# Four of sixteen DMA engines for 256 columns of a weight block, and a result in 16 rows

## The chip, the cores and the metric

The kernel runs on one core of one Trainium2 chip. The metric is the device time of one execution in microseconds; runs are compared by the median. A core has engines that run side by side and wait for one another by semaphores: TensorE (PE, its weight loads shown as PEld), VectorE (DVE), ScalarE (ACT), GpSimd (POOL) and SyncE (SP), which here issues the loads and the store. Transfers are carried by 16 DMA engines. SBUF is the memory of 128 partitions that they fill; PSUM is the memory that TensorE accumulates in.

## The reference

One token, with a gate between an attention block and a gated feed-forward block. All is float32.

```
g = sigmoid(sum(x * gate_w))
a = attention(x @ wq, k_cache, v_cache) @ wo      # 32 query heads, 4 key/value heads, 65536 positions
r = x @ w_r
b = x + sigmoid(r) * ((silu(x @ w_gate) * (x @ w_up)) @ w_down)
out = g * a + (1 - g) * b                          # 1024 numbers
```

With one token the router's choice is always that token. D is 1024, the feed-forward width F is 3584, so `w_down` has 3584 rows of 1024 columns.

## The kernel before

The data are read once, in the order of use, through three SBUF buffers `st` of 128 partitions by 64 KB. For each of four key/value heads there are nine loads of 8 MB (part of `wq`, the keys, the values, part of `wo`); then six loads of 7 MB hold `w_gate`, `w_up` and `w_down`. SP issues a load as soon as the buffer it goes to is free, so the DMA queue always has the next loads in it.

The last two buffers come in pieces, each with a semaphore of its own, so that TensorE can begin on a piece before the rest has landed. `ENDS` lists the columns at which pieces end, in units of D = 1024 columns for one block of `w_down`. The last buffer holds blocks 14 to 27: pieces of six blocks, four, two (24 and 25), one (26), then 768 and 256 columns of block 27. Each piece is one DMA of all 128 partitions (line 132). In SBUF the partition p of block b holds row 32 b + p mod 32 of the p // 32-th quarter of `w_down`'s rows.

TensorE works in column groups of 32: four matmuls that write PSUM partitions 0, 32, 64 and 96 on. `hp` is the transposed hidden vector, 32 columns for each block, of which the first has the numbers. Blocks 0 to 23 are added up in the bank `att` (line 392), 512 columns a matmul; after the mark "early" VectorE adds `att` to the attention part in `att_sb` (line 277). The last four blocks (24 to 27, from `EARLY` on) go to banks `y` and `acc` (line 409): `PIECES` splits each quarter of 256 columns into 192 and 64, and a block has four matmuls of 192 columns into `y` and four of 64 into `acc`, one for each group of 32 partitions. In block 26 the matmuls of line 404 add `att_sb` to the same banks, with the weight `halves` that sums the groups; before them TensorE waits for VectorE's sum. The host lays block 27 out so that its first 768 columns hold the `y` part of all four quarters and its last 256 the `acc` part.

When the 192-column part of block 27 is done (mark "first"), ScalarE copies `y` to `fin` (line 182); when the rest is done (mark "last"), VectorE copies `acc` to `fin` (line 280). SP waits for both, stores `fin` as four rows of 256 numbers, from partitions 0, 32, 64 and 96 (line 136), waits until the store has landed, and clears the semaphores.

Instructions of TensorE are laid out in a straight line, but for a loop over the four heads. A matmul of the program appears in the profile as two MATMUL and two LDWEIGHTS records.

Of the kernel before, what the change touches and what calls it, by code (L numbers as in the profile page):

```python
# [4 lines left out]
AF = mybir.ActivationFunctionType  # L5
# [3 lines left out]
P = 128  # L9
D = 1024  # L10
G = 4
# [3 lines left out]
F = 3584  # L15
CH = 8192
NCH = SK // CH
NM = CH // 512
NB = CH // P
KB = D // P  # L20
NQ = D // 4
FB = F // P
FN = F // 8
SCALE = DH ** -0.5
# [3 lines left out]
PER = UNITS // 2  # L28
BUFS = 3

TAIL = 14336
NTAIL = 3 * KB * F // TAIL

ENDS = {NTAIL - 2: [8 * D, TAIL], NTAIL - 1: [6 * D, 10 * D, 12 * D, 13 * D, 13 * D + 768, TAIL]}

PIECES = [(0, 192), (192, NQ)]

EARLY = 24


HEAD = ["q", "qt"] + [f"s{c}" for c in range(NCH)] + ["mx"] + [f"v{c}" for c in range(NCH)] + ["o", "w"]
MARKS = ["dot"] + [f"{m} {g}" for g in range(G) for m in HEAD]
MARKS += ["gate 0", "gate 1", "up 0", "up 1", "early", "first", "last"]
MARK = {m: i + 1 for i, m in enumerate(MARKS)}

LAST = ["s0", "s2", "s4", "s6", "v0", "v2", "v4", "v6", "w"]

ACTS = ["sig"] + [f"{m}{c} {g}" for g in range(G) for m in "se" for c in range(NCH)] + ["hid", "first"]
ACTED = {m: i + 1 for i, m in enumerate(ACTS)}


def gated_mix_kernel(nc, x, vecs, heads, ffn, out):

# [18 lines left out]
    pe, act, dve, pool, sp = nc.tensor, nc.scalar, nc.vector, nc.gpsimd, nc.sync  # L74

    stream = [nc.alloc_sbuf_tensor(f"st{b}", [P, 2 * CH], F32, align_bytes=256)[:, :] for b in range(BUFS)]
    scores = nc.alloc_sbuf_tensor("s", [P, NCH, 512], F32)[:, :, :]
    pts = nc.alloc_sbuf_tensor("pt", [P, 2, 512], F32)[:, :, :]

    hid = scores[:, 0:2, :].rearrange("p a n -> p (a n)")[:, : FB * 32]  # L80
    hp = scores[:, 2:4, :].rearrange("p a n -> p (a n)")[:, : FB * 32]
    att_sb = scores[:, 4, :]
    zeros = scores[:, 5, :]
    fin = scores[:, 7, :NQ]

    o_sb = scores[:, 0, :].rearrange("p (s d) -> p s d", s=4)
    q_sb, lb = scores[:, 1, :], scores[:, 2, :P]
# [1 line left out]
    def sb(name, *shape):  # L89
        t = nc.alloc_sbuf_tensor(name, [P, *shape], F32)  # L90
        return t[tuple(slice(None) for _ in range(len(shape) + 1))]
# [1 line left out]
    xk = sb("xk", 3, KB)  # L93
    x_row, ident, ones, md = sb("x_row", 2 * NQ), sb("ident", P), sb("ones", P), sb("md", P)
    sel, sel8, nsel, sel4 = sb("sel", 32), sb("sel8", HG), sb("nsel", HG), sb("sel4", 4)
    half, halves = sb("half", 2), sb("halves", 2, 32)
    xp, qp, op = sb("xp", KB, 32), sb("qp", 4 * (32 + HG)), sb("op", HG, 32)
    dots, dsum, sig, rest = sb("dots", 2, KB), sb("dsum", 2), sb("sig", 2), sb("rest", 2)
    mx, sums, mh, rl = sb("mx", NCH), sb("sums", NCH), sb("mh", HG), sb("rl", HG)
    m1, nb, l1 = sb("m1", 1), sb("nb", 1), sb("l1", 1)  # L100
    gate = sig[:, 0:1]

    def psum(name, *shape):
        return nc.alloc_psum_tensor(name, [P, *shape])[tuple(slice(None) for _ in range(len(shape) + 1))]

    ps_u, ps_f = psum("ps_u", 2, 512), psum("ps_f", 2, 512)
    ps_s = [ps_u[:, i, :] for i in range(2)]
    acc, ps_m, att, y = psum("acc", 512), psum("ps_m", P), psum("att", 512), psum("y", NQ)

    banks = [y, acc]  # L110

    names = ["done", "fed", "x0", "x1", "x2", "acted", "pooled", "marked", "d2p", "d2a", "d2s", "self"]
    names += [f"ld{b}" for b in range(BUFS)] + [f"end{i}" for i in range(sum(map(len, ENDS.values())))]
    sems = {n: nc.alloc_semaphore(n) for n in names}
# [4 lines left out]
    ends = []  # L119
    for i in range(G * PER + NTAIL):  # L120
        b = i % BUFS
        if i >= BUFS:
            g, l = divmod(i - BUFS, PER)
            sp.wait_ge(sems["marked"], MARK[f"{LAST[l]} {g}" if g < G else ["gate 0", "gate 1", "up 0"][l]])
        if i < G * PER:
            sp.dma_start(stream[b], heads[i]).then_inc(sems[f"ld{b}"], 16)
        elif i - G * PER not in ENDS:
            sp.dma_start(stream[b][:, :TAIL], ffn[i - G * PER]).then_inc(sems[f"ld{b}"], 16)
        else:
            cuts = ENDS[i - G * PER]  # L130
            for c0, c1 in zip([0] + cuts, cuts):
                sp.dma_start(stream[b][:, c0:c1], ffn[i - G * PER, :, c0:c1]).then_inc(sems[f"end{len(ends)}"], 16)  # L132
                ends.append((i, c0, c1))
    sp.wait_ge(sems["acted"], ACTED["first"])
    sp.wait_ge(sems["d2s"], 1)
    sp.dma_start(
        out.rearrange("(j n) -> j n", j=4), fin[::32, :]
    ).then_inc(sems["done"], 16)
    sp.wait_ge(sems["done"], 16)
    sp.sem_clear(range(nums[0], nums[-1] + 1))  # L140

# [4 lines left out]
    for t in (xp, qp, zeros, halves, op):  # L146
# [4 lines left out]
        out=ident, in_=ident, compare_op=ALU.not_equal, fill=1.0, base=0, pattern=[[-1, P]], channel_multiplier=1  # L151
# [3 lines left out]
    acted = []  # L155

    def tell(ins, name):
        acted.append(name)
        return ins.then_inc(sems["acted"])
# [17 lines left out]
            )  # L177
    act.wait_ge(sems["marked"], MARK["gate 1"])
    tell(act.activation(hid.rearrange("p (e n) -> p e n", e=2), ps_f[:, :, :FN], AF.Exp, scale=-1.0), "hid")  # L179
    act.wait_ge(sems["marked"], MARK["first"])  # L180
    c0, c1 = PIECES[0]
    tell(act.activation(fin[:, c0:c1], banks[0][:, : c1 - c0], AF.Copy), "first")
    assert acted == ACTS


# [35 lines left out]
    then(dve.tensor_copy(sel4, ident.rearrange("p (j h) -> p j h", h=32)[:, :, 0]))  # L221

    then(dve.tensor_add(half, sel4[:, :2], sel4[:, 2:]))
    dve.tensor_copy(halves[:, :, 0], half)
    then(dve.tensor_reduce(sel8, ident.rearrange("p (a h) -> p h a", h=HG), AX.X, ALU.add))
    then(dve.tensor_scalar_mul(nsel, sel8, -SCALE))
    for g in range(G):
# [10 lines left out]
        for c in range(NCH):  # L238
            acted_on(f"s{c} {g}")
            ins = dve.tensor_reduce(mx[:, c : c + 1], scores[:, c, :], AX.X, ALU.max)  # L240
# [35 lines left out]
    after("early")  # L276
    to_pe(dve.tensor_add(att_sb, att, att_sb))
    after("last")
    c0, c1 = PIECES[1]
    dve.tensor_copy(fin[:, c0:c1], banks[1][:, : c1 - c0]).then_inc(sems["d2s"])  # L280


    marks = []
# [1 line left out]
    def mark(ins, name):  # L285
        marks.append(name)
        ins.then_inc(sems["marked"])
# [17 lines left out]
    with pe.Fori(0, G):  # L305
        loaded(0)
        for k in range(KB):
            for f in range(2):
                j = 2 * (k % 2) + f
                ins = pe.matmul(  # L310
                    ps_s[0][32 * j : 32 * j + 32, :], xp[:, k, :],
                    unit(0)[:, k * D + f * 512 : k * D + (f + 1) * 512], start=(k < 2), stop=(k >= KB - 2),
                )
        mark(ins, "q")
        take("d2p")
        for e in range(4):
            ins = pe.matmul(ps_m[:, 2 * e : 2 * e + 2], q_sb[:, e * DH : (e + 1) * DH], half, start=True, stop=True)
        mark(ins, "qt")
        take("d2p")
        for c in range(NCH):  # L320
# [3 lines left out]
            for s in range(4):  # L324
                for j in range(4):
                    ins = pe.matmul(  # L326
                        ps_s[c % 2][32 * j : 32 * j + 32, :], qp[:, 32 * s : 32 * s + 32],
                        unit(1 + c)[:, (4 * s + j) * 512 : (4 * s + j + 1) * 512], start=(s == 0), stop=(s == 3),
                    )
# [3 lines left out]
        for c in range(NCH):  # L333
            loaded(1 + NCH + c)
            take("d2p")
            for m in range(NM):
                j = m % 4
                ins = pe.matmul(  # L338
                    acc[32 * j : 32 * j + 32, :], pts[:, c % 2, 32 * m : 32 * m + 32],
                    unit(1 + NCH + c)[:, m * 512 : (m + 1) * 512], start=(c == 0 and m < 4),  # L340
                    stop=(c == NCH - 1 and m >= NM - 4),
                )
# [3 lines left out]
        for s in range(4):  # L346
            ins = pe.matmul(
                ps_m[:, HG : 2 * HG], o_sb[:, s, :], sel[:, HG * s : HG * s + HG], start=(s == 0), stop=(s == 3)
            )
        mark(ins, "o")  # L350
        take("d2p")
        for h in range(HG):
            for f in range(2):
                j = 2 * (h % 2) + f
                ins = pe.matmul(  # L355
                    att[32 * j : 32 * j + 32, :], op[:, h, :],
                    unit(UNITS - 1)[:, h * D + f * 512 : h * D + (f + 1) * 512], start=False, stop=False,
                    skip_group_check=True,
                )
# [4 lines left out]
    def tail(first, n):  # L364
        i, c = divmod(first, TAIL)
        assert c + n <= TAIL
        if i < min(ENDS):
            if c == 0:
                take(f"ld{(G * PER + i) % BUFS}", 16)
        else:  # L370
            for e, (i1, c0, _) in enumerate(ends):
                if (i1 - G * PER, c0) == (i, c):
                    pe.wait_ge(sems[f"end{e}"], 16)
        return stream[(G * PER + i) % BUFS][:, c : c + n]


    for i, part in enumerate(("gate", "up")):
        ps = (ps_f, ps_u)[i]
        for k in range(KB):
            for e in range(2):  # L380
                for j in range(4):
                    ins = pe.matmul(  # L382
                        ps[32 * j : 32 * j + 32, e, :FN], xp[:, k, :], tail((i * KB + k) * F + (2 * j + e) * FN, FN),
                        start=(k == 0), stop=(k == KB - 1),
                    )
# [3 lines left out]
    for b in range(EARLY):  # L389
        for f in range(2):  # L390
            j = 2 * (b % 2) + f
            ins = pe.matmul(  # L392
                att[32 * j : 32 * j + 32, :], hp[:, 32 * b : 32 * b + 32], tail(2 * KB * F + b * D + f * 512, 512),
                start=(b < 2), stop=(b >= EARLY - 2),
            )
    mark(ins, "early")
    for b in range(EARLY, FB):
        if b == EARLY + 2:
            take("d2p")
        for bank, (c0, c1) in zip(banks, PIECES):  # L400
            n = c1 - c0
            for j in range(4):
                if b == EARLY + 2:
                    pe.matmul(  # L404
                        bank[32 * j : 32 * j + 32, :n], halves[:, j // 2, :],
                        att_sb[:, j % 2 * NQ + c0 : j % 2 * NQ + c1], start=False, stop=False,
                    )
                at = 4 * c0 + j * n if b == FB - 1 else j * NQ + c0
                ins = pe.matmul(  # L409
                    bank[32 * j : 32 * j + 32, :n], hp[:, 32 * b : 32 * b + 32], tail(2 * KB * F + b * D + at, n),  # L410
                    start=(b == EARLY), stop=(b == FB - 1),
                )
            if b == FB - 1:
                mark(ins, "first" if c0 == 0 else "last")
    assert marks == MARKS


# [29 lines left out]
```

## Time and profile before

| what | value |
|---|---|
| median of 3 runs | 805.84 us (805.73 to 806.34) |
| profiled execution | 805.78 us |
| its span, first to last instruction | 804.5 us |
| PE busy | 407.5 us, 51% of the span |
| DVE busy | 72.3 us, 9% |
| ACT busy | 44.8 us, 6% |
| DMA | 346.20 MB, mean 430 GB/s |
| granted TensorE clock, mean | 0.75 of full |

The page is of one profiled execution; its time is a little longer than its span, since the time counts what lies before the first and after the last instruction. Busy shares tell little alone: the engine or queue that is behind at the end of a chain of waits sets the time. Three views are used below. The timeline lists groups of instructions: start, duration, engine, line, operation, the tiles it writes and reads, its shapes, the count, and in brackets the idle time before and what ended it. The view of windows gives for each stretch the busy time of PE, PEld, DVE, ACT and POOL, the granted clock, the share of the 16 DMA engines that is busy, and GB/s. The DMA view gives for a stretch, by queue, the packets that start in it, their megabytes, and their time as a share of 16 engines over the stretch; in a stretch shorter than a packet that share can be far over 100%. A DMA of many rows becomes packets, one for each row, and one tiny packet on each engine that tells of its completion. The queue q1 carries SP's loads and the store, q10 the two small loads at the start, and q8 fetches instructions.

### The profile page before, as it was taken

How to read it: one execution, taken by the hardware profiler on the slowest of the kernel's cores; microseconds unless marked ns; L12 is line 12 of the kernel's file. 1: busy time of each engine (PE TensorE's matmuls, PEld its weight loads, DVE VectorE, ACT ScalarE, POOL GpSimd, SP SyncE). 2: the span in 40 equal slices, each digit the busy share in tenths (PEclk: the TensorE clock that was granted, in tenths of full speed). 3: DMA queues.
4: the chain of work that ended last, by engine and by line, in shares of the span. 5: the costliest groups of instructions: out<-in, count | busy, mean ns of one | idle time of the engine just before them, and what ended most of it. 6: DMA issues, size and time to landing. Idle time of an engine off the chain costs nothing. (4 is left out here: it accounts for less than half of the span.)

```text
span 804.5 us, 6124 instructions
## 1 busy us (share of the span) xinstructions
PE 407.5 (51%) x2826; PEld 122.0 (15%) x2826; DVE 72.3 (9%) x135; ACT 44.8 (6%) x100; POOL 2.5 (0%) x13
## 2 busy tenths in 40 slices
PE   0544464455654564545544454456444545464466
PEld 0211111111111121111111111112111111121122
DVE  0200010000000020000100110000000100000310
ACT  0000030000000030000000110000000300000000
POOL 1000000000000000000000000000000000000000
PEclk9977767768767677677877586777776866787778
DMA  9999999999999999999999999999999999999998
GB/s 418 417 418 466 415 424 460 417 428 453 420 430 450 424 431 446 427 430 446 427 430 443 430 430 443 430 431 430 440 433 427 443 430 430 429 448 426 439 413 342
DMA packets 7078, 346.20 MB, mean 430 GB/s; under 512 B 918, under 2 KB 1050, under 8 KB 1308
## 3 DMA queue, kind: packets, MB, share of 16 engines
q1 hardware_dynamic: 6920, 346.04, 99.4%
q8 instruction: 8, 0.13, 0.1%
q10 hardware_dynamic: 148, 0.02, 0.0%
q14 instruction: 2, 0.02, 0.0%
HBM read 346.05 MB, written 0.00 MB: 430 GB/s over the span
## 5 line engine op out<-in xcount | busy, mean ns | idle before, releaser
L326 PE MATMUL ps_u<-st,qp 128*32 128x512 f32 x1024 | 152.5, 759 | 149.1 <-PEq L290 149.1
L338 PE MATMUL acc<-st,pt 128*32 128x512 f32 x1024 | 152.3, 757 | 144.1 <-PEq L290 144.1
L338 PEld LDWEIGHTS acc<-st,pt 128*32 128x32 f32 x1024 | 43.5, 135 | 250.0 <-issue 250.0
L326 PEld LDWEIGHTS ps_u<-st,qp 128*32 128x32 f32 x1024 | 41.4, 135 | 256.3 <-issue 256.3
L171 ACT ACTIVATE s<-ps_u 128x512 f32<-128x512 f32 x32 | 19.1, 597 | 560.4 <-PE ps_u L326 560.4
L240 DVE TENSOR_REDUCE mx<-s 128x1 f32<-128x512 f32 x32 | 22.0, 686 | 284.2 <-ACT s L171 284.2
L255 DVE STREAM_TRANSPOSE pt<-s 128x512 f32<-128x512 f32 x32 | 22.7, 711 | 198.0 <-PE acc L338 194.4
L310 PE MATMUL ps_u<-st,xp 128*32 128x512 f32 x128 | 23.3, 893 | 22.1 <-PEq L290 22.1
L382 PE MATMUL ps_u<-st,xp 128*32 128x448 f32 x128 | 17.1, 703 | 16.9 <-PEq L290 16.9
L382 PE MATMUL ps_f<-st,xp 128*32 128x448 f32 x128 | 16.8, 691 | 13.3 <-PEq L290 13.3
L176 ACT ACTIVATE s<-s,nb 128x512 f32<-128x512 f32 x32 | 22.6, 708 | 10.4 <-DVE nb L250 10.4
L392 PE MATMUL att<-st,s 128*32 128x512 f32 x96 | 14.9, 776 | 7.5 <-DMA st<-in_ffn 4.9
L355 PE MATMUL att<-st,op 128*32 128x512 f32 x128 | 14.6, 594 | 2.4 <-PEq L290 2.4
L301 PE MATMUL ps_m<-dsum,ones 128*128 128x2 f32 x2 | 0.6, 350 | 23.5 <-PEq L290 23.5
L310 PEld LDWEIGHTS ps_u<-st,xp 128*32 128x32 f32 x128 | 5.9, 158 | 40.1 <-issue 40.1
L382 PEld LDWEIGHTS ps_u<-st,xp 128*32 128x32 f32 x128 | 5.3, 139 | 28.6 <-issue 28.6
L259 DVE COPY s<-acc 128x512 f32<-128x512 f32 x4 | 2.8, 692 | 71.6 <-PE acc L338 71.6
L382 PEld LDWEIGHTS ps_f<-st,xp 128*32 128x32 f32 x128 | 5.2, 135 | 25.1 <-issue 25.1
L229 DVE COPY s<-ps_u 128x512 f32<-128x512 f32 x4 | 2.8, 692 | 53.5 <-PE ps_u L310 53.5
L179 ACT ACTIVATE s<-ps_f 128x896 f32<-128x896 f32 x1 | 0.9, 917 | 105.4 <-PE ps_f L382 105.4
L392 PEld LDWEIGHTS att<-st,s 128*32 128x32 f32 x96 | 3.7, 134 | 18.6 <-issue 10.7
L332 PE MATMUL ps_m<-md,ones 128*128 128x128 f32 x8 | 1.8, 311 | 8.2 <-PEq L290 8.2
(69 smaller groups left out, 68.9 us busy)
## 6 DMA issues: line engine op xcount, KB each, us to landing
st<-in_ffn SPq DMA_DIRECT2D x4, 7168.0 KB, 43.3
st<-in_ffn SPq DMA_DIRECT2D x2, 3072.0 KB, 37.1
st<-in_ffn SPq DMA_DIRECT2D x1, 4096.0 KB, 34.9
st<-in_ffn SPq DMA_DIRECT2D x1, 2048.0 KB, 36.9
st<-in_ffn SPq DMA_DIRECT2D x1, 1024.0 KB, 38.9
st<-in_heads SPq DMA_DIRECT2D x36, 48.1
st<-in_ffn SPq DMA_DIRECT2D x1, 512.0 KB, 39.7
st<-in_ffn SPq DMA_DIRECT2D x1, 384.0 KB, 40.2
```

Source lines behind the costliest of these rows:

```text
L171: tell(act.activation(scores[:, c, :], ps_s[c % 2], AF.Copy), f"s{c} {g}")
L176: act.activation(t, t, AF.Exp, bias=nb, scale=SCALE, accum_out=sums[:, c : c + 1]), f"e{c} {g}"
L229: to_pe(dve.tensor_copy(q_sb, ps_s[0]))
L240: ins = dve.tensor_reduce(mx[:, c : c + 1], scores[:, c, :], AX.X, ALU.max)
L255: to_pe(dve.transpose(pts[:, c % 2, :], scores[:, c, :]))
L259: to_pe(dve.tensor_copy(o_sb, acc.rearrange("p (s d) -> p s d", s=4)))
L310: ins = pe.matmul(ps_s[0][32 * j : 32 * j + 32, :], xp[:, k, :], unit(0)[:, k * D + f * 512 : k * D + (f + 1) * 512], start=(k < 2), stop= ...
L326: ins = pe.matmul(ps_s[c % 2][32 * j : 32 * j + 32, :], qp[:, 32 * s : 32 * s + 32], unit(1 + c)[:, (4 * s + j) * 512 : (4 * s + j + 1) * ...
L338: ins = pe.matmul(acc[32 * j : 32 * j + 32, :], pts[:, c % 2, 32 * m : 32 * m + 32], unit(1 + NCH + c)[:, m * 512 : (m + 1) * 512], start= ...
L355: ins = pe.matmul(att[32 * j : 32 * j + 32, :], op[:, h, :], unit(UNITS - 1)[:, h * D + f * 512 : h * D + (f + 1) * 512], start=False, sto ...
L382: ins = pe.matmul(ps[32 * j : 32 * j + 32, e, :FN], xp[:, k, :], tail((i * KB + k) * F + (2 * j + e) * FN, FN), start=(k == 0), stop=(k == ...
L392: ins = pe.matmul(att[32 * j : 32 * j + 32, :], hp[:, 32 * b : 32 * b + 32], tail(2 * KB * F + b * D + f * 512, 512), start=(b < 2), stop= ...
```

## The change

The last buffer is cut otherwise. `ENDS` now has pieces of six blocks, four blocks, the first 768 columns of block 24, its last 256 columns, two blocks (25 and 26), and 768 and 256 columns of block 27. The 256 columns of block 24 (`NARROW`) come by two DMAs with one semaphore, of partitions 0 to 123 and of partitions 124 to 127 (`ROWS`); TensorE waits for 32 on it.

The result is summed in one bank `y` of 64 columns. A block now has 16 matmuls of 64 columns: for c in 0 to 3 and each of the four groups of partitions. The weight is the same 32-column window of `hp`, moved by 8 c columns, so that the numbers come to partition 32 j + 8 c. `halves` becomes 64 columns wide with its numbers in column 32, and is moved in the same way. The 16 matmuls that add `att_sb` stand before block 25, behind the wait for VectorE's sum. ScalarE's copy, the mark "first" and one of SP's waits go; VectorE copies 64 columns of `y`; the store has 16 rows of 64 numbers, from every eighth partition. The host lays block 27 out in 16 runs of 64 columns.

```
-ENDS = {NTAIL - 2: [8 * D, TAIL], NTAIL - 1: [6 * D, 10 * D, 12 * D, 13 * D, 13 * D + 768, TAIL]}
-PIECES = [(0, 192), (192, NQ)]
+ENDS = {NTAIL - 2: [8 * D, TAIL], NTAIL - 1: [6 * D, 10 * D, 11 * D - NQ, 11 * D, 13 * D, 13 * D + 12 * NR, TAIL]}
+NARROW, ROWS = (NTAIL - 1, 11 * D - NQ), [(0, 124), (124, P)]
...
-                sp.dma_start(stream[b][:, c0:c1], ffn[i - G * PER, :, c0:c1]).then_inc(sems[f"end{len(ends)}"], 16)
+                for r0, r1 in ROWS if (i - G * PER, c0) == NARROW else [(0, P)]:
+                    sp.dma_start(
+                        stream[b][r0:r1, c0:c1], ffn[i - G * PER, r0:r1, c0:c1]
+                    ).then_inc(sems[f"end{len(ends)}"], 16)
                 ends.append((i, c0, c1))
-    sp.wait_ge(sems["acted"], ACTED["first"])
     sp.wait_ge(sems["d2s"], 1)
-    sp.dma_start(
-        out.rearrange("(j n) -> j n", j=4), fin[::32, :]
-    ).then_inc(sems["done"], 16)
+    sp.dma_start(out.rearrange("(i n) -> i n", i=16), fin[::8, :]).then_inc(sems["done"], 16)
...
-    act.wait_ge(sems["marked"], MARK["first"])
-    c0, c1 = PIECES[0]
-    tell(act.activation(fin[:, c0:c1], banks[0][:, : c1 - c0], AF.Copy), "first")
...
-    dve.tensor_copy(halves[:, :, 0], half)
+    dve.tensor_copy(halves[:, :, 32], half)
...
-    c0, c1 = PIECES[1]
-    dve.tensor_copy(fin[:, c0:c1], banks[1][:, : c1 - c0]).then_inc(sems["d2s"])
+    dve.tensor_copy(fin, y).then_inc(sems["d2s"])
...
-                    pe.wait_ge(sems[f"end{e}"], 16)
+                    pe.wait_ge(sems[f"end{e}"], 16 * len(ROWS) if (i, c) == NARROW else 16)
...
     for b in range(EARLY, FB):
-        if b == EARLY + 2:
+        if b == EARLY + 1:
             take("d2p")
-        for bank, (c0, c1) in zip(banks, PIECES):
-            n = c1 - c0
+            for c in range(4):
+                for j in range(4):
+                    pe.matmul(
+                        y[32 * j : 32 * j + 32, :], halves[:, j // 2, 32 - 8 * c : 64 - 8 * c],
+                        att_sb[:, j % 2 * NQ + c * NR : j % 2 * NQ + (c + 1) * NR], start=False, stop=False,
+                    )
+        for c in range(4):
             for j in range(4):
-                if b == EARLY + 2:
-                    pe.matmul(
-                        bank[32 * j : 32 * j + 32, :n], halves[:, j // 2, :],
-                        att_sb[:, j % 2 * NQ + c0 : j % 2 * NQ + c1], start=False, stop=False,
-                    )
-                at = 4 * c0 + j * n if b == FB - 1 else j * NQ + c0
+                at = 4 * c + j if b == FB - 1 else 4 * j + c
                 ins = pe.matmul(
-                    bank[32 * j : 32 * j + 32, :n], hp[:, 32 * b : 32 * b + 32], tail(2 * KB * F + b * D + at, n),
-                    start=(b == EARLY), stop=(b == FB - 1),
+                    y[32 * j : 32 * j + 32, :], hp[:, 32 * b - 8 * c : 32 * b - 8 * c + 32],
+                    tail(2 * KB * F + b * D + at * NR, NR), start=(b == EARLY and c == 0),
+                    stop=(b == FB - 1 and c == 3),
                 )
-            if b == FB - 1:
-                mark(ins, "first" if c0 == 0 else "last")
+    mark(ins, "last")
```

More of the change, by code (lines that the diff above doesn't have):

```diff
@@ L21 @@
 NQ = D // 4
+NR = NQ // 4
 FB = F // P
@@ L42 @@
 MARKS = ["dot"] + [f"{m} {g}" for g in range(G) for m in HEAD]
-MARKS += ["gate 0", "gate 1", "up 0", "up 1", "early", "first", "last"]
+MARKS += ["gate 0", "gate 1", "up 0", "up 1", "early", "last"]
 MARK = {m: i + 1 for i, m in enumerate(MARKS)}
 LAST = ["s0", "s2", "s4", "s6", "v0", "v2", "v4", "v6", "w"]
-ACTS = ["sig"] + [f"{m}{c} {g}" for g in range(G) for m in "se" for c in range(NCH)] + ["hid", "first"]
+ACTS = ["sig"] + [f"{m}{c} {g}" for g in range(G) for m in "se" for c in range(NCH)] + ["hid"]
 ACTED = {m: i + 1 for i, m in enumerate(ACTS)}
@@ L83, in gated_mix_kernel @@
     zeros = scores[:, 5, :]
-    fin = scores[:, 7, :NQ]
+    fin = scores[:, 7, :NR]
     o_sb = scores[:, 0, :].rearrange("p (s d) -> p s d", s=4)
@@ L95, in gated_mix_kernel @@
     sel, sel8, nsel, sel4 = sb("sel", 32), sb("sel8", HG), sb("nsel", HG), sb("sel4", 4)
-    half, halves = sb("half", 2), sb("halves", 2, 32)
+    half, halves = sb("half", 2), sb("halves", 2, 64)
     xp, qp, op = sb("xp", KB, 32), sb("qp", 4 * (32 + HG)), sb("op", HG, 32)
@@ L107, in gated_mix_kernel @@
     ps_s = [ps_u[:, i, :] for i in range(2)]
-    acc, ps_m, att, y = psum("acc", 512), psum("ps_m", P), psum("att", 512), psum("y", NQ)
-    banks = [y, acc]
+    acc, ps_m, att, y = psum("acc", 512), psum("ps_m", P), psum("att", 512), psum("y", NR)
     names = ["done", "fed", "x0", "x1", "x2", "acted", "pooled", "marked", "d2p", "d2a", "d2s", "self"]
@@ L430 @@
     down = a["B_w_down"].reshape(4, FB, 32, D).transpose(0, 2, 1, 3).reshape(P, FB, D).copy()
-    last = down[:, -1].reshape(P, 4, NQ)
-    down[:, -1] = np.concatenate([last[:, :, c0:c1].reshape(P, -1) for c0, c1 in PIECES], axis=1)
+    down[:, -1] = down[:, -1].reshape(P, 4, 4, NR).transpose(0, 2, 1, 3).reshape(P, D)
     ffn = np.concatenate([t.reshape(P, -1) for t in (a["B_w_gate"], a["B_w_up"], down)], axis=1)
```

## The prediction

> **What bounds the kernel now.** I read the page's first three parts, then the end of the chain of waits, the timeline of the last 8 us, and the DMA view over ever smaller windows.
>
> ```profile
> span 804.5 us, 6124 instructions
> ...
> DMA  9999999999999999999999999999999999999998
> ...
> q1 hardware_dynamic: 6920, 346.04, 99.4%
> q8 instruction: 8, 0.13, 0.1%
> ```
>
> The load queue (q1) keeps the 16 DMA engines busy for 99.4% of the span, so all of it is a stream of 346 MB, and only what the stream takes, or what follows its last byte, is in the time. The chain says the same, then a short tail:
>
> ```profile
> 760.52 38.89 DMA st<-in_ffn
> ...
> 802.20 0.16 PE acc L409 x8
> 802.36 0.02 issue
> 802.38 0.23 DVE s L280
> ```
>
> The timeline of the tail shows which piece each group of matmuls waited for:
>
> ```profile
> 799.01 0.69 DVE L277 TENSOR_TENSOR s<-att,s 128x512 f32<-128x512 f32 x1 [20.00 <-PE att L392]
> 799.46 0.53 PE L409 MATMUL y<-st,s 128*32 128x192 f32 x8 [0.51 <-DMA st<-in_ffn]
> ...
> 799.80 0.29 PE L409 MATMUL acc<-st,s 128*32 128x64 f32 x8
> ...
> 799.92 0.51 PE L409 MATMUL y<-st,s 128*32 128x192 f32 x8
> ...
> 800.72 0.11 PEld L409 LDWEIGHTS y<-st,s 128*32 128x32 f32 x1 [0.26 <-DMA st<-in_ffn]
> ...
> 801.67 0.53 PE L409 MATMUL y<-st,s 128*32 128x192 f32 x8
> ...
> 802.02 0.29 PE L409 MATMUL acc<-st,s 128*32 128x64 f32 x8
> 802.27 0.33 ACT L182 ACTIVATE s<-y 128x192 f32<-128x192 f32 x1 [58.66 <-PE y L409]
> 802.38 0.23 DVE L280 COPY s<-acc 128x64 f32<-128x64 f32 x1 [2.68 <-PE acc L409]
> 802.70 0.63 SPq L136 DMA_DIRECT2D out<-s  x1
> ```
>
> A piece lands about 0.05 us before the matmuls that it releases: the 1 MB of blocks 24 and 25 at 799.4, block 26 at 800.7, the first 768 columns of block 27 at 801.6, the last 256 columns some 0.3 us on, 801.9. From the last matmuls (802.02) on the tail is fixed: copy, store, end at 804.5.
>
> A landing is that of the slowest engine, and the engines don't end together:
>
> ```profile
> 799.80:800.20 0.40, 0.40 (x24) 0.36 (x16) 0.00 (x0) 0.00 (x0) 0.00 (x0) 1.00 0.88 341
> 800.20:800.60 0.40, 0.40 (x18) 0.23 (x8) 0.00 (x0) 0.00 (x0) 0.00 (x0) 1.00 0.58 228
> 800.60:801.00 0.40, 0.40 (x10) 0.26 (x12) 0.00 (x0) 0.00 (x0) 0.00 (x0) 1.00 0.49 195
> 801.00:801.40 0.40, 0.40 (x18) 0.34 (x11) 0.00 (x0) 0.00 (x0) 0.00 (x0) 1.00 0.41 146
> 801.40:801.80 0.40, 0.40 (x24) 0.39 (x19) 0.00 (x0) 0.00 (x0) 0.00 (x0) 1.00 0.25 77
> ```
>
> The last columns are the granted clock, the DMA share and GB/s. From 800.2 the share falls to 0.58, then 0.49 and 0.41: of 16 engines about nine, eight and seven still move data. Seven to nine have nothing left for up to 1.6 us before the end; the others set it. The window from 801.36 to 801.65 counts the late ones, since an engine ends each piece with one tiny packet:
>
> ```profile
> DMA packets 28, 0.04 MB, mean 125 GB/s; under 512 B 7, under 2 KB 27, under 8 KB 27
> ```
>
> Seven such packets: seven late engines. Why they are late is seen where an instruction fetch (16 KB, q8) meets a load. The rows are the windows 46.35 to 46.45, 47.305 to 47.315 and, undisturbed, 48.35 to 48.37:
>
> ```profile
> q8 instruction: 1, 0.02, 57.8%
> ...
> q1 hardware_dynamic: 1, 0.07, 1828.1%
> ...
> q1 hardware_dynamic: 1, 0.07, 755.6%
> ```
>
> A share times its window times 16 is a packet's time: 0.92 us for the fetch, 2.93 us for the 64 KB packet that follows, against 2.42 us for an undisturbed one. That packet starts at 47.31, 0.91 us behind the fetch, and takes 0.51 longer: one fetch puts one engine back by 1.4 us. Eight fetches, the last at 801.4 when little was left, and seven late engines: each fetch hit another engine.
>
> **The change part by part.** The stream's order and bytes stay. What moves is which engine carries 128 KB of it: 128 rows of 1 KB, 256 columns of block 24, now in DMAs of 124 and of four rows. How many engines these use is to be read from DMAs of few rows. The two-row load of x (window 24.49 to 24.60) and the four-row store (803 to 804.5):
>
> ```profile
> q10 hardware_dynamic: 2, 0.00, 9.3%
> ...
> DMA packets 8, 0.00 MB, mean 3 GB/s; under 512 B 4, under 2 KB 8, under 8 KB 8
> ```
>
> Two packets for two rows, and four packets with four completions for four: an equal share of rows for each engine, at most 16 engines. 124 is four times 31, with no other even split between four and 16, so I take four engines of 31 rows, and the same four with one row each. Bounds: all 16 (nothing changes), or one engine with all 128.
>
> [...]
>
> The price of a row is in the window 801.465 to 801.535, where only 1 KB packets start:
>
> ```profile
> q1 hardware_dynamic: 4, 0.00, 16.4%
> ```
>
> 16.4% of 70 ns on 16 engines is 184 ns, 46 ns for each of four packets, overlapping slightly. The last piece, eight rows an engine, takes 0.3 us, which is 38 ns a row. The four engines carry 32 rows instead of eight: 24 more, 0.9 (38 ns) to 1.1 us (46 ns); I take 1.0. The other twelve carry eight rows less: 0.3 us sooner from there on. If the four are among those that end 1.0 us or more before the last, the landing of every later piece comes 0.3 us sooner.
>
> Which engines these are, the profile doesn't number. Followed from packet to packet (each begins as the one before ends), the two engines of the two-row load are not among those that a q8 fetch hit, as far as packets a few ns apart can be told apart. [...] I take it that the four have the room.
>
> *Issue.*
>
> ```profile
> 759.67 2.70 SPq L132 DMA_DIRECT2D st<-in_ffn  x6
> ```
>
> SP issues eight DMAs where there were these six, two more of 0.45 us each. They stand in one stretch near 760, and the last landed 39 us later (the chain's DMA step), so this hides behind the queue; without that cover it would be 0.9 us. Nothing else waits behind them on SP but the store.
>
> *Matmuls.* The row starts give 0.46 us for a block of four matmuls of 192 and four of 64 columns (799.46 to 799.92), and 0.12 us for four of 64 (799.80 to 799.92). A block is now 16 of 64: four sets, 0.48 us, 0.02 more. The 16 matmuls that add the attention part replace eight, again 0.48 for 0.46, and stand before block 25 instead of inside block 26. They wait for VectorE's sum (799.70); behind them wait blocks 25 to 27. The new 2 MB piece (blocks 25 and 26) lands with the old block 26 less 0.3, at 800.4, so these 0.48 us have 0.7 to fit in; without this cover they cost up to 0.5. Then blocks 25 and 26 run in one go, 0.96 us from 800.43 to 801.39; the 768-column piece is there at 801.35, three sets end at 801.75; the last piece is there at 801.6. So the last four start at 801.75 instead of 802.02, 0.27 sooner: TensorE is just behind the loads, as it was. All of this is at clock 1.00.
>
> *Copies.* ScalarE's copy goes; it ended at 802.60, VectorE's at 802.61, and that one stays 64 columns wide: 0 to 0.02. The wider zeroed weight and its memset lie at the start, under the first load.
>
> *Store.* 16 rows of 256 B for four of 1 KB; by the split above it uses 16 engines. No row shows such a store. Below: packets shorter by 0.03. Above: 16 engines that start from rest, as in the first load, between 1.70 and 2.75, eight of them by 1.90:
>
> ```profile
> DMA packets 8, 0.52 MB, mean 2621 GB/s; under 512 B 0, under 2 KB 0, under 8 KB 0
> ...
> DMA packets 16, 1.05 MB, mean 999 GB/s; under 512 B 0, under 2 KB 0, under 8 KB 0
> ```
>
> Their first packets spread over up to 1.05 us, so up to +0.9. The store has one small packet an engine and its nearest row, the four-row store, is quick: I take +0.1. [...]
>
> *Sum* against the profiled execution, 805.78 us (span 804.5, the rest around it), 0.06 below the median 805.84: 805.78 − 0.27 + 0.1 = 805.6; with the offset, 805.7. From 805.3 (no store cost, full 0.3) to 806.1.
>
> **The rivals.**
> *The four include a late engine.* Then the narrow piece's 1.0 us is put on top of its lateness and all later pieces land that much later: 805.8 + 1.0 + 0.1 = 806.9. For it: seven of 16 are late, and blind chance would seldom leave four free (nine of 16, eight of 15, seven of 14, six of 13: 7%). Against it: the followed pair. Between lie one or two engines that end 0.7 to 0.9 us before the last (the steps from 0.49 to 0.41): with one of these among the four the gain goes, 805.9 to 806.1.
>
> *A fetch lands elsewhere.* TensorE now has twice the matmuls in the last four blocks, so the instruction at which the eighth fetch was sent (801.4, in block 26) is passed in or just behind block 24, about 1.5 us sooner, while data still flow. If it hits one of the four, that engine carries 1.0 and 1.4 us extra on 1.6 of room: the landing comes some 0.8 later, 806.7; on a late engine 1.4 later, 807.3. It decides from the point where the fetch starts before its engine's last packet. Against it: seven fetches went to seven engines, so the eighth should hit one that is early, and most of those aren't among the four.
>
> *It doesn't split as said.* On 16 engines nothing moves: 805.8 to 805.9. On one engine, 128 rows at 38 to 46 ns are 4.9 to 5.9 us, eight rows of which it had before; less 1.6 of room, +3 to +4: about 809.
>
> **How the numbers follow.** Forecast 0.50 (a third of it with the gain lost to a middling engine), late engine among the four 0.24, fetch 0.10, no split 0.06, one engine 0.05, store near its upper bound 0.05 (806.4). Range 805.3 to 807.0: it holds the forecast, the late engine and the dear store, and leaves out most of the fetch on a late engine and the one engine. A measurement of this kernel tells 0.2%, 1.6 us, from no change: faster means under 804.2, which no case reaches (0.03 for a thing not thought of), slower over 807.5, the one-engine case and sums of two others: 0.10. The rest, 0.87, is within.
>
> **What would show it.** Right: four engines seen working alone on 1 KB packets some 2 to 3 us before the end; the DMA share staying near 0.9 up to 801 and falling within half a microsecond; the last matmuls starting near 801.75; from the store's issue to the end the same 1.8 us. Wrong: the share at 0.25 or less for over a microsecond at the end, with the last matmuls past 802.5 (late engine or fetch; a q8 packet before 800.5 tells the second), or the narrow piece landing after the pieces behind it.

## The result, and the profile after

The changed kernel takes 807.45 us (median of 22 runs, 806.48 to 808.09) beside 805.84 us before (22 runs, 805.63 to 806.34). The ratio is 1.0018, with a 95% interval of 1.0013 to 1.0024: slower by 1.6 us, just under the 0.2% that the prediction took as its bound, and above its range. The profiled execution took 807.86 us.

The page's first lines of the changed kernel:

```profile
span 806.5 us, 6284 instructions
...
DMA  9999999999999999999999999999999999999997
...
q1 hardware_dynamic: 7080, 346.04, 99.3%
q8 instruction: 8, 0.13, 0.1%
```

The stream has as many bytes as before, is as dense, and meets eight instruction fetches as before. The 2.0 us that the span has gained are at the end. The chain of waits of the changed kernel (start, duration, what):

```profile
773.11 28.56 DMA st<-in_ffn
801.67 0.04 issue
801.72 1.38 PE y L406 x78
803.10 0.87 issue
803.96 0.51 PE y L406 x18
804.47 0.02 issue
804.50 0.23 DVE s L277
```

Two things are new. The piece of blocks 25 and 26 releases TensorE at 801.72, where 800.43 was forecast. And after 78 of the 96 matmul records of blocks 25 to 27 TensorE stands still for 0.87 us on "issue": it waits for nothing that the profile shows. Record 78 is in the middle of a set of four matmuls, where the program has no wait. VectorE's copy starts at 804.50 where it was 802.38. From the store's issue (804.75) to the end it takes 1.8 us, as before.

The view of windows of the changed kernel, at its end; the last three columns are granted clock, DMA share, GB/s:

```profile
801.40:801.80 0.40, 0.08 (x5) 0.08 (x9) 0.00 (x0) 0.00 (x0) 0.00 (x0) 1.00 0.60 215
801.86:802.16 0.30, 0.30 (x32) 0.30 (x30) 0.00 (x0) 0.00 (x0) 0.00 (x0) 1.00 0.13 48
802.16:802.50 0.34, 0.34 (x40) 0.34 (x32) 0.00 (x0) 0.00 (x0) 0.00 (x0) 1.00 0.07 24
```

Shares of 0.13 and 0.07 are two engines of 16, then one. The other fourteen have ended by 801.87; before, the last of all was through at 801.65, some 0.2 us sooner. So two engines end later than anything did, and the rest have not become earlier.

### The profile page after: what moved, and what is told of

Read it like the earlier page. It is cut to its first block, busy times and chain, and to the rows that moved or that the text cites. A ratio compares the mean times of both kernels' runs of the same rounds, so it can differ in the third digit from the quotient of the medians.

```text
span 806.5 us, 6284 instructions
## 1 busy us (share of the span) xinstructions
PE 399.9 (50%) x2906; PEld 121.3 (15%) x2906; DVE 72.4 (9%) x135; ACT 44.5 (6%) x99; POOL 2.6 (0%) x13
## 5 line engine op out<-in xcount | busy, mean ns | idle before, releaser
L323 PE MATMUL ps_u<-st,qp 128*32 128x512 f32 x1024 | 148.8, 743 | 154.8 <-PEq L287 154.8
L335 PE MATMUL acc<-st,pt 128*32 128x512 f32 x1024 | 149.9, 747 | 146.5 <-PEq L287 146.5
L352 PE MATMUL att<-st,op 128*32 128x512 f32 x128 | 16.3, 652 | 2.4 <-PEq L287 2.4
L352 PEld LDWEIGHTS att<-st,op 128*32 128x32 f32 x128 | 4.9, 117 | 10.4 <-issue 10.4
```

Source lines behind the costliest of these rows:

```text
L323: ins = pe.matmul(ps_s[c % 2][32 * j : 32 * j + 32, :], qp[:, 32 * s : 32 * s + 32], unit(1 + c)[:, (4 * s + j) * 512 : (4 * s + j + 1) * ...
L335: ins = pe.matmul(acc[32 * j : 32 * j + 32, :], pts[:, c % 2, 32 * m : 32 * m + 32], unit(1 + NCH + c)[:, m * 512 : (m + 1) * 512], start= ...
L352: ins = pe.matmul(att[32 * j : 32 * j + 32, :], op[:, h, :], unit(UNITS - 1)[:, h * D + f * 512 : h * D + (f + 1) * 512], start=False, sto ...
```

## The experiments

All runs are compared with the kernel before on the same chip. "Split" stands for the two DMAs of the narrow piece, "pause" for TensorE's stop on "issue" in block 27. A run with fewer causes than the changed kernel is to be read beside the two ends, 805.9 and 807.45.

| run | split 124+4 | pause | median, us | range | before, same chip | ratio, 95% interval |
|---|---|---|---|---|---|---|
| e1 one DMA | no | yes | 806.47 | 806.23 to 806.90 | 805.97 | 1.0007, 0.9997 to 1.0016 |
| e2 split in the kernel before | yes | no | 806.75 | 806.55 to 807.35 | 805.97 | 1.0011, 1.0002 to 1.0020 |
| e3 no pause | yes | no | 806.53 | 806.20 to 807.06 | 805.97 | 1.0007, 0.9998 to 1.0016 |
| e4 one DMA, no pause | no | no | 805.95 | 805.71 to 806.18 | 805.97 | 0.9998, 0.9989 to 1.0007 |
| e5 block 24 early | no | no | 806.30 | 806.07 to 806.79 | 805.85 | 1.0006, 0.9997 to 1.0015 |
| e6 lower and upper half | no | no | 812.91 | 812.72 to 814.67 | 805.85 | 1.0095, 1.0079 to 1.0110 |
| e7 even and odd | no | no | 805.78 | 805.62 to 805.96 | 805.85 | 0.9999, 0.9990 to 1.0008 |
| e9 narrow piece in halves | 64+64 | no | 806.31 | 805.97 to 806.67 | 805.90 | 1.0005, 0.9996 to 1.0014 |
| e10 512 columns | yes | no | 809.34 | 808.31 to 809.75 | 805.90 | 1.0037, 1.0024 to 1.0051 |
| e11 128 columns | yes | no | 805.91 | 805.71 to 806.43 | 805.90 | 1.0001, 0.9992 to 1.0010 |

e8, with the split and a pause, was executed once: 807.09 us. The intervals reach 0.7 us and more to either side, further than most of these runs lie apart; what decides are e1 to e4, which ran side by side on one chip, and the profiles. All eleven executions of e4 (806.18 us at most) are shorter than the shortest of e1, e2 and e3 (806.20).

### e1: one DMA instead of two

```
-NARROW, ROWS = (NTAIL - 1, 11 * D - NQ), [(0, 124), (124, P)]
+NARROW, ROWS = (NTAIL - 1, 11 * D - NQ), [(0, P)]
```

> The changed kernel with the 256 columns of block 24 in one DMA of 128 rows again; matmuls and store as changed. My theory has two causes, each of about 1 us: the split delays the last landing (803.0 for 801.9), and TensorE then runs out of instructions in block 27 (idle from 802.9 to 804.0, in the middle of a set that waits for no load) because its doubled matmuls reach a block of instructions that is still being fetched. So here the last piece lands at 801.8 to 802.2 again, the pause in block 27 stays, and the time is 806.6 to 807.5. Rival, the split alone does it all (the pause too, since the fetch waits on an engine that the split has loaded): 805.7 to 806.0, no pause.

It took 806.47 us, a little under the range of my theory and well over the rival's. The pause is there without the split. Timeline of TensorE in e1:

```profile
801.09 1.34 PE L406 MATMUL y<-st,s 128*32 128x64 f32 x78 [0.25 <-DMA st<-in_ffn]
802.75 0.49 PE L406 MATMUL y<-st,s 128*32 128x64 f32 x18 [0.32 <-issue]
```

The same 78 and 18 records with "issue" between them, but 0.32 us long where it was 0.87. Why it is shorter shows in the last fetch. The first row is the changed kernel's, in a window of 5 ns from 801.350; the second is e1's, in a window of 10 ns from 800.555:

```profile
q8 instruction: 1, 0.02, 1582.5%
...
q8 instruction: 1, 0.02, 576.2%
```

1582.5% of 5 ns on 16 engines is 1.27 us, 576.2% of 10 ns 0.92 us. With the split the fetch begins at 801.35 instead of 800.56 and takes 0.35 us longer. TensorE goes on 1.3 us after the fetch has ended in both: 801.35 + 1.27 to 803.96, 800.56 + 0.92 to 802.75.

### e2: the split alone, in the kernel before

```
-ENDS = {NTAIL - 2: [8 * D, TAIL], NTAIL - 1: [6 * D, 10 * D, 12 * D, 13 * D, 13 * D + 768, TAIL]}
+ENDS = {NTAIL - 2: [8 * D, TAIL], NTAIL - 1: [6 * D, 10 * D, 11 * D - NQ, 11 * D, 13 * D, 13 * D + 768, TAIL]}
+NARROW, ROWS = (NTAIL - 1, 11 * D - NQ), [(0, 124), (124, P)]
...
-                sp.dma_start(stream[b][:, c0:c1], ffn[i - G * PER, :, c0:c1]).then_inc(sems[f"end{len(ends)}"], 16)
+                for r0, r1 in ROWS if (i - G * PER, c0) == NARROW else [(0, P)]:
+                    sp.dma_start(
+                        stream[b][r0:r1, c0:c1], ffn[i - G * PER, r0:r1, c0:c1]
+                    ).then_inc(sems[f"end{len(ends)}"], 16)
...
-                    pe.wait_ge(sems[f"end{e}"], 16)
+                    pe.wait_ge(sems[f"end{e}"], 16 * len(ROWS) if (i, c) == NARROW else 16)
```

> The kernel before with the changed cut of the last buffer and the two DMAs of 124 and four rows; its matmuls of 192 and 64 columns, two copies and four-row store stay. My theory: the last landing is 0.7 to 1.1 us later, no pause of TensorE: 806.5 to 806.9. Rival, the split is hidden or gains and the matmuls and the store do it all: 805.4 to 806.0. Rival, the split does it all: 807.2 to 807.7.

806.75 us, in the first range: 0.8 us over before, with the old matmuls, copies and store. The new cut has a part in it: block 25 now lands with block 26, so that the matmuls of blocks 25 to 27 and the additions among them all stand behind one landing (801.35), where before blocks 24 and 25 were released at 799.46. What the split alone costs is better read from e3 and e4. The copy of `acc` starts at 803.40 (802.38 before), and no matmul waits on "issue":

```profile
803.40 0.23 DVE L285 COPY s<-acc 128x64 f32<-128x64 f32 x1 [3.38 <-PE acc L414]
```

### e3 and e4: the same program 24 matmuls further on

```
-    for j in range(4):
-        pe.matmul(att[32 * j : 32 * j + 32, :], op[:, 0, :], zeros, start=True, stop=False, skip_group_check=True)
+    for j in range(28):
+        pe.matmul(att[32 * (j % 4) : 32 * (j % 4) + 32, :], op[:, 0, :], zeros, start=True, stop=False, skip_group_check=True)
```

> The changed kernel with 24 more matmuls that zero the bank att once more, at the start, under the first load; nothing else differs. They move every later matmul 24 places on in the program, so that a bound between blocks of instructions, which I put at matmul 247 or so behind the loop, comes at about 223, in block 26, and its fetch is asked for about 24 matmuls sooner, well before the last loads. My theory: no pause in block 27, landing late as in the changed kernel: 806.4 to 807.0. Rival, the pause comes from the late loads, the shifted weight windows or PSUM and not from fetching: the pause stays at the same matmul, 807.2 to 807.7.

> Both at once: one DMA of 128 rows, and the 24 matmuls at the start. My theory: what is left of the change (64-column matmuls in one bank, one copy, the store of 16 rows) costs little: 805.6 to 806.1. Rival, the store or the matmuls cost by themselves: 806.3 or more.

Both came as my theory had them: 806.53 and 805.95 us. Adding work at the start, where TensorE waits anyway, takes 0.9 us off the changed kernel. One fetch still starts between 795 and 805 in e3, and takes about 1.1 us (q8 has 0.7% of that stretch); at which time, that view doesn't tell. All 96 records run in one go:

```profile
801.65 1.59 PE L406 MATMUL y<-st,s 128*32 128x64 f32 x96 [0.47 <-DMA st<-in_ffn]
```

The changed kernel, e1, e3 and e4 make a square. Split without pause costs 0.58 us (e3 less e4), pause without split 0.52 (e1 less e4), both together about 1.5 (the changed kernel less e4, from different chips, whose kernel before differs by 0.1). The two are not independent: the split makes the pause longer, as the fetch in e1 showed. e4 has all the rest of the change and stands at the time of before.

The DMA view of e3 and of e4, both over 795 to 805, also tells how many engines a DMA of 124 rows uses:

```profile
DMA packets 780, 2.43 MB, mean 243 GB/s; under 512 B 120, under 2 KB 376, under 8 KB 632
```

```profile
DMA packets 796, 2.56 MB, mean 256 GB/s; under 512 B 128, under 2 KB 384, under 8 KB 640
```

An engine ends its part of a DMA with one packet under 512 B: the kernel before has 6920 packets on q1, of which 48 loads of 128 rows and the store of four make 6148, and 16 for each load and four for the store the other 772. e4 has 128 packets of that size here: 16 for each of six loads, 16 for the store, and the store's own 16 rows of 256 B. e3 has 120: the 16 of the narrow piece are replaced by eight, four for each of its two DMAs if the four rows go to four engines, as those of the store before did.

### e8: four matmuls further on

The edit is that of e3 with 8 in place of 28.

> The changed kernel with four more zeroing matmuls at the start (24 in the run without a pause). If the pause stands at a bound between blocks of instructions, it comes four matmuls sooner in the program: before it 70 of the 96 matmul records of blocks 25 to 27, for 78 in the changed kernel, and it ends a little sooner, as its fetch is asked for sooner. Rival, the pause belongs to the place in the sum or to the loads: 78 records again.

The pause moved by eight records, and became short. TensorE in e8:

```profile
801.38 1.21 PE L406 MATMUL y<-st,s 128*32 128x64 f32 x70 [0.51 <-DMA st<-in_ffn]
802.76 0.61 PE L406 MATMUL y<-st,s 128*32 128x64 f32 x26 [0.18 <-issue]
```

70 and 26, for 78 and 18: so the pause stands at a place in the program's instructions, not in the sum or the loads.

### e5: no narrow piece, and fewer matmuls

```
-ENDS = {NTAIL - 2: [8 * D, TAIL], NTAIL - 1: [6 * D, 10 * D, 11 * D - NQ, 11 * D, 13 * D, 13 * D + 12 * NR, TAIL]}
-NARROW, ROWS = (NTAIL - 1, 11 * D - NQ), [(0, 124), (124, P)]
-EARLY = 24
+ENDS = {NTAIL - 2: [8 * D, TAIL], NTAIL - 1: [6 * D, 10 * D, 11 * D, 13 * D, 13 * D + 12 * NR, TAIL]}
+NARROW, ROWS = (-1, 0), [(0, P)]
+EARLY = 25
```

> The changed kernel with no narrow piece (block 24 is one piece, one DMA) and with block 24 among the early blocks, two matmuls of 512 columns in place of 16 of 64: 14 matmuls fewer, 242 behind the loop, so the program should end before the bound at about 247. My theory: neither cause is left, no pause in block 27, 805.6 to 806.1. Rival, the pause comes from dense 64-column matmuls in three blocks and not from fetching: a pause of 0.3 us or more in block 27, 806.3 to 806.6.

806.30 us, outside the range of my theory and in the rival's, but not for its reason, as no pause on "issue" is to be seen. The timeline of e5 shows another cause:

```profile
800.52 0.69 DVE L275 TENSOR_TENSOR s<-att,s 128x512 f32<-128x512 f32 x1 [22.47 <-PE att L389]
...
801.36 0.65 PE L399 MATMUL y<-s,halves 128*32 128x64 f32 x32
801.80 1.10 PE L406 MATMUL y<-st,s 128*32 128x64 f32 x64
802.97 0.22 DVE L277 COPY s<-y 128x64 f32<-128x64 f32 x1 [1.75 <-PE y L406]
```

With block 24 among the early ones VectorE's sum starts at 800.52, 1.5 us later than before. The edit also moves the 16 matmuls of line 399, which stand before block `EARLY` + 1, behind block 25, and so behind the landing of blocks 25 and 26 at about 800.7. They start at 801.36, when block 25 is through; the sum was there at 801.21. So they no longer fit in before the loads. The run is 0.45 us over before; the prediction had put these matmuls at up to 0.5 "without this cover".

### e6 and e7: what half of the partitions costs

In the kernel before, the 2 MB piece of blocks 20 to 23 in two DMAs of 64 partitions each, halves in e6 (shown) and every second partition in e7:

```
-                sp.dma_start(stream[b][:, c0:c1], ffn[i - G * PER, :, c0:c1]).then_inc(sems[f"end{len(ends)}"], 16)
+                for rows in [slice(0, 64), slice(64, P)] if (i - G * PER, c0) == (NTAIL - 1, 6 * D) else [slice(0, P)]:
+                    sp.dma_start(
+                        stream[b][rows, c0:c1], ffn[i - G * PER, rows, c0:c1]
+                    ).then_inc(sems[f"end{len(ends)}"], 16)
...
-                    pe.wait_ge(sems[f"end{e}"], 16)
+                    pe.wait_ge(sems[f"end{e}"], 32 if (i, c) == (NTAIL - 1, 6 * D) else 16)
```

> The kernel before, with the 2 MB piece (blocks 20 to 23) in two DMAs, of partitions 0 to 63 and 64 to 127. Each of the 16 engines carries four rows of each, as many bytes as before. What this tells apart is why the split slows every engine and not only its four. Theory A, what is limited is the way into SBUF, by partition: with half the partitions as the target the 16 engines share half the ways in, and each half takes twice its time: 4 to 5 us longer in all, 810 to 811, with packets of 16 KB taking about 1.2 us for 0.61. Theory B, the limit is each engine, and small packets or reads are what slowed the others: 805.6 to 806.3.

> As the run with halves, but of even and of odd partitions, so that each of the two DMAs reaches over all partitions while an engine again carries four rows of each. Both theories: no more than 0.5 us over before, 805.6 to 806.4. If this one is as slow as the halves, DMAs of 64 rows cost by themselves and the halves tell nothing of the way into SBUF.

e6 takes 812.91 us, 7.1 us more, over theory A's range but on its side (where the 2 us beyond the range come from is not shown); e7 takes 805.78, no more than before. Windows of e6, then of e7:

```profile
786.00:790.00 4.00, 2.00 (x20) 0.39 (x12) 0.00 (x0) 0.00 (x0) 0.00 (x0) 1.00 0.98 424
792.00:794.00 2.00, 0.00 (x0) 0.00 (x0) 0.00 (x0) 0.00 (x0) 0.00 (x0) 0.80 1.10 229
794.00:796.00 2.00, 1.94 (x12) 0.59 (x16) 0.00 (x0) 0.00 (x0) 0.00 (x0) 0.50 0.89 221
```

```profile
792.00:794.00 2.00, 1.91 (x12) 0.60 (x16) 0.00 (x0) 0.00 (x0) 0.00 (x0) 0.50 0.96 410
794.00:796.00 2.00, 2.00 (x19) 0.32 (x8) 0.00 (x0) 0.00 (x0) 0.00 (x0) 0.69 1.01 430
```

In e6 all engines are busy (shares near 1) and move 229 and 221 GB/s, about half of 424. In e7, with as many DMAs, rows and bytes, it is 410 and 430. What differs is which partitions a DMA writes. The rows that are read from memory change along with them, so that it is the writing that slows, and not the reading, is not shown apart.

### e9, e10 and e11: the narrow piece in halves, doubled and halved

All three are e3 with one edit: e9 has `ROWS = [(0, 64), (64, P)]`, e10 the narrow piece from `11 * D - 2 * NQ`, e11 from `11 * D - NQ // 2`.

> The run without a pause (24 zeroing matmuls at the start), its 256 columns of block 24 in DMAs of partitions 0 to 63 and 64 to 127 instead of 124 and four rows: all 16 engines carry eight rows as ever, only the target is half of the partitions at a time. My theory, that the way into SBUF goes by partition, loses about the piece's own time once more, 0.3 us: 806.1 to 806.4, beside 805.95 with one DMA and 806.53 with 124 and four rows. Rival, what costs is that four engines carry the piece, and no more: 805.8 to 806.05.

> The run without a pause, with 512 columns of block 24 by DMAs of 124 and four rows: twice the load on the four engines. My theory: the ways into SBUF of the other engines gain nothing, and the end is set by those of the four that were not early, each carrying 2.0 us more where it was 1.0: about 0.9 to 1.3 us over the run with 256 columns (806.53), so 807.4 to 807.9. Rival, the small packets slow all engines alike: in proportion, twice the 0.55 us, so 806.9 to 807.2. Rival, the split costs by itself, whatever its size: 806.4 to 806.7.

> The same with 128 columns: half the load on the four engines, 0.5 us more for each. My theory: the engines of the four that end 0.7 us before the last have room for it, so nearly nothing is lost and nothing gained: 805.8 to 806.1. Rival, in proportion: 806.2 to 806.3. If moving load to early engines gains at all, this run is the one that would show it: under 805.7.

e9: 806.31 us, 0.4 over before, with eight rows for every engine if 64 rows go evenly to 16, which fits a cost of where the data go without any uneven load; its interval (0.9996 to 1.0014) does not exclude no cost. e11: 805.91, no loss and, against what the prediction would have it, no gain, though each of the four engines has only half of the extra bytes. e10: 809.34, 2.8 over e3 and more than any of the three expectations. Part of that is another thing. Windows of e10:

```profile
800.00:803.00 3.00, 1.09 (x60) 0.93 (x60) 0.39 (x1) 0.00 (x0) 0.00 (x0) 1.00 0.72 264
803.40:806.40 3.00, 2.79 (x96) 2.54 (x96) 0.03 (x1) 0.00 (x0) 0.00 (x0) 0.50 0.06 18
```

The 96 records start at 803.5, 1.9 us later than in e3, and take 2.79 us at a granted clock of 0.50 for 1.59 us at 1.00. So in the profiled execution the load costs 1.9 us more than in e3, and the clock 1.2. From 128 over 256 to 512 columns the loss against before goes 0, 0.6, and about 2.2 without the clock (809.34 − 805.90 − 1.2): not in proportion to the columns, as if there were room for the first of them.

The timelines show the same without pause, clock or store: from the first weight load of blocks 20 to 23 to that of blocks 25 to 27, each of which waits for a landing, it takes 3.6 us in e11, 3.7 in e4, 4.0 in e9, 4.2 in e3 and in the changed kernel, and 5.8 in e10. So in its one trace e9 does lose some 0.3 us of the stream.

## Why the prediction was wrong, point by point

- *The stream bounds the kernel, its last landing and a fixed tail make the time.* Right, up to the last landing; the tail behind it was not fixed.
- *124 rows go to four engines.* Right, by the count of completion packets in e3 and e4 (120 for 128). Followed from packet to packet in the changed kernel, four engines carry 31 rows of 1 KB each, and then one more.
- *The four have the room.* This step failed. Two followed engines spoke for it, and no row for all four. The last 0.6 us of the changed kernel's stream are carried by two engines and then by one. The profile doesn't number engines, but followed from packet to packet these two are of the four: they ended the piece of blocks 20 to 23 at 795.93 and 796.26, where the last engine ended it at 796.86, so they had 0.9 and 0.6 us of room, and the narrow piece took each of them 1.1 to 1.2 us more than eight rows of 1 KB took an engine before (0.34 us). The other two of the four had 1.4 us of room and ended in time. The rival between, "one or two engines that end 0.7 to 0.9 us before the last", is what came, at several times its price: the split alone costs 0.6 us (e3 less e4), not 0.1 to 0.3.
- *The other twelve come 0.3 us sooner.* This failed too, and it was the whole of the expected gain. Followed in the same way, these engines take 2.7 to 2.8 us from the end of block 24's first 768 columns to that of blocks 25 and 26 in the changed kernel, with no narrow rows of their own. Before, an engine's eight packets of 8 KB took 2.45 us (blocks 24 and 25) and eight rows of 1 KB 0.34, together 2.8: what they were relieved of, they lost again. The sum took an engine's time for the limit. In e6 and e7 the rate goes by the partitions that are written: 221 to 229 GB/s with 64 neighbouring ones at a time, 410 to 430 with every second one. That fits, as an inference: rows that the four engines carry go to the same partitions as before, and so would slow the engines that write there. What the engines share on the way into SBUF no run shows. In the windows from 797.2 to 799.1, of the changed kernel and of e4, the first moves less with as busy engines (e3, on the chip of e4, 361):

```profile
797.20:799.10 1.90, 1.58 (x16) 0.54 (x19) 0.00 (x0) 0.00 (x0) 0.00 (x0) 1.00 1.06 363
```

```profile
797.20:799.10 1.90, 1.90 (x20) 0.54 (x20) 0.00 (x0) 0.00 (x0) 0.00 (x0) 0.97 1.04 429
```

- *A row costs 38 to 46 ns.* Near. From packet to packet the four took 1.3 to 1.5 us for 31 rows, 43 to 47 ns a row, so the price of 1.0 us for 24 rows was at most 0.2 too low. What failed is the room that it was held against.
- *The last four matmuls start at 801.75, TensorE just behind the loads.* Failed by a cause that the sum didn't hold. The sum had the matmuls' time nearly right (1.59 us for the 48 matmuls of three blocks, 0.53 a block, where 0.48 was taken), but not that 40 more matmuls are more instructions (the page counts 6284 for 6124). The fetch rival saw that the eighth fetch would matter; it charged the fetch to the data of the engine it hits, and not to TensorE, which, by e3 and e8, stands still at a place that goes with the count of instructions. Nor did the fetch come 1.5 us sooner, as that rival had it, but at 801.35, where it was 801.41. Before, with 40 matmuls fewer, no such pause is seen.
- *Issue: two more DMAs of 0.45 us, hidden.* Hidden, but mis-sized. SP's timeline in the changed kernel:

```profile
759.53 31.69 SPq L134 DMA_DIRECT2D st<-in_ffn  x8
```

The eight issues take 31.7 us, not 3.6; the last ends at 791.2, and the first of its data move at 800.0. The cover held with some 9 us to spare, and e11, with an issue as long, takes no more time than before. e1, with one DMA, took 3.18 us for seven.
- *Store +0.1, copies 0.* Near: 1.8 us from issue to end in both, and e4 stands at the time of before.

The premise that each fetch had made another engine late holds for the first two, in the kernel before: the 16 completion packets of the load that ends at 41 us lie within 0.6 us; behind the first fetch (46.4) 15 of the next load's do and one comes over 1 us later; behind the second (87.5) 14 do and two come late.

The changed kernel's 1.6 us are thus the split, about 0.6 (e3 less e4), and the pause, 0.9 (the changed kernel less e3). No run beat the kernel before beyond its spread: e7, e4 and e11 equal it.

## What to carry to other kernels

Before load is moved from late DMA engines to early ones, ask what the limit is: here the rate went by the partitions that were written, and the engines that were relieved came no sooner, so a load spread unevenly lost (0.6 us, e3 less e4), or at best (e11) gained nothing that the time shows. DMAs whose 64 rows lay all over the partitions lost nothing (e7, 805.78 us), those that went to 64 neighbouring ones lost 7.1 us (e6); the count of rows also went with how many engines a DMA used, 16 for 128 rows, four for 124 and for four. And where the last stretch of a kernel is dense with short instructions, look at their number as a cost of its own: here 40 more matmuls came with a standstill of 0.87 us near an instruction fetch, and 24 idle ones at the start took it away.

## What the runs showed of the hardware that was not expected

- DMAs that wrote to 64 neighbouring partitions moved 221 to 229 GB/s (e6), to every second partition 410 to 430 (e7). What slows the first no run shows.
- TensorE stood still for 0.18 (e8), 0.32 (e1) and 0.87 us (the changed kernel) on nothing that the profile names, at a place that moved with the count of instructions ahead of it (78 records, 70 after four more matmuls, no pause after 24). In e1 and the changed kernel it went on 1.3 us after a 16 KB fetch had ended. That the fetch brings its own instructions is an inference from that.
- One issue of a DMA on SP took up to 13.7 us in the changed kernel, where the median was 0.43 us. The row is the view by line, with shortest, median and longest in ns:

```profile
L134 SPq DMA_DIRECT2D st<-in_ffn x10: 327/433/13708, 742.6 to 777.5; - x10
```

Such issues came in every run in which this line issues ten DMAs, and in none with nine or eight (e1, e4 to e7, 0.59 us at most; before, 0.86). e9, whose ten are all of 64 or 128 rows, had one of 10.8 us, and the changed kernel, with 124 and four, three:

```profile
L134 SPq DMA_DIRECT2D st<-in_ffn x2: 3877/7838/11800, 761.3 to 773.1; - x2
```

This is the same view between 764 and 776.9: 11.8 and 3.9 us come ahead of the 13.7. So the count of DMAs that the line issues goes with the wait, and the kind of the split with its length. What the issue waits for was not tried.
- In e10 the last matmuls ran at a granted clock of 0.50, after TensorE had waited for the loads; in the changed kernel they ran at 1.00. Whether the wait is the cause was not tried.
